# Decay attention and two expert layers: output products grouped by array tiling, a head pair's states stacked in 64 columns

## Chip, cores and metric

One core of one Trainium2 chip. The metric is device microseconds for one execution of the whole program. Before the change: median 974.29 us of 3 runs (974.17 to 976.9).

## The reference, cut to what matters

```python
# q, k, v, alpha: (batch 4, heads 8, seq 768, head_dim 48)
for t in range(S):
    state = alpha[:, :, t, :, None] * state + einsum('bhd,bhde', k[:, :, t], v[:, :, t])
    y[:, :, t] = einsum('bhd,bhde->bhe', q[:, :, t], state)
x = y.transpose(0, 2, 1, 3).reshape(3072, 384)
h = x @ w_in                                   # 384 -> 2048
x = (max(h, 0) + alpha_moe * min(h, 0)) @ w_out
h = x @ w_in2                                  # second layer, another activation g
out = g(h) @ w_out2
```

The weights arrive as float64. The expert layers multiply in two-part float32r words; the attention multiplies in float32.

## The kernel before, in words

**Attention.** The 768 tokens of a batch are cut into six chunks of 128 tokens (`CPB`), 24 chunks in all (`NCH`), numbered c = 0 to 23. A chunk holds all 8 heads, as 4 pairs (`NP`): the first head of a pair stands on partitions 0 to 47, the second on 64 to 111 (`HALVES`), and 48 to 63 and 112 to 127 are padding. Per chunk there are these parts:

- `fetch(c)`: q, k and the decays, transposed so that features stand on partitions, into `T`. Chunks 0 to 9 are transposed on TensorE (L195). Later ones are transposed on VectorE in blocks of 32 (`X`, L205), and sixteen DMAs put the blocks in place (`T<-X`, L211); then `load_chunk` loads the next chunk's inputs (L157).
- `at_alpha`: two scans over the decays, one backward (`R`, L221) and one forward (`F`, L226). `at_qk`: `K2` and `Q2`.
- `at_scores`: `sc`, one product a head with 48 rows (L247), masked into `A` by VectorE (L252), and `kt`, the transposed keys (L258), copied to `KT` by ScalarE (L260).
- `at_out`: the output `y` of the chunk, `[128, 4 pairs, 128 tokens]` in one PSUM tile. For each pair it is the product of the state `bd` with `Q2` (L271, left out in the first chunk of a batch) and for each head of the pair the product of `v` with `A` (L274). `bd` is block diagonal, 128 rows by 128 columns a pair, so that one product serves both heads. `ds` is the chunk's addition to the state (L288, left out in a batch's last chunk). ScalarE and VectorE then split `y` into the two float32r parts of `xs` (L300 to L307), and VectorE adds `ds` to `bd` (`state()`, L313 or L315), one instruction for each half. Six DMAs put the last pair's rows into the padding of the other three pairs (`xs<-x`, L323).
- `at_decay`: GpSimd multiplies `bd` by the next chunk's decays (L332), one instruction for each half.

**Startup.** Chunks 0 to 3, whose outputs are the first block of 512 tokens, run before any expert product. There `at_out` makes pair 3 first, ScalarE copies it (`y3`, L280), and three products with `sel` (L295) put its rows into the other pairs' padding, each behind its own pair. `mid()` stands between: ScalarE's copy of a weight (`split_hi`, L407).

**Expert layers.** Six blocks of 512 tokens for each layer, 16 steps (fc) a block: step s emits `hp` (L429, 9 products), the activation on VectorE and ScalarE (L444 to L452), the low part `gl` on GpSimd (L453), and then step s-1's output products (`o`, L462, 9 products in layer 0; `y`, L473 in layer 1). In the first block each step also loads, converts and splits a weight (VectorE `wf`, L366 and L368; ScalarE `wst`, L360 and L361).

**Order.** Every engine runs its instructions in the order in which the program emits them (`tc.manual_schedule`). After each step `run_slots` emits the next group of attention work: at_out(c-1); at_qk, at_decay and fetch; at_alpha; at_scores. Four steps make a chunk, so the attention of block j+1 is spread over block j, and the first `hp` of a block needs the last `xs` of its four chunks. All DMAs are issued by SyncE, one queue in program order.

The lines of `at_out` and `at_decay` that the change touches:

```python
        def emit_y(p, done=True):
            if not first:
                nc.tensor.matmul(out=y[:, p, :], lhsT=bd[:, p, :], rhs=s["Q2"][:, p, :],
                                 start=True, stop=False)
            for a in range(2):
                nc.tensor.matmul(out=y[64 * a:64 * a + 64, p, :], lhsT=vc[:, 2 * p + a, :],
                                 rhs=s["A"][a][:, p, :], start=first, stop=done)
```

Of the kernel before, what the change touches and what calls it, by code (L numbers as in the profile page):

```python
# [7 lines left out]
F32 = mybir.dt.float32  # L8
# [14 lines left out]
def kernel(  # L23
# [13 lines left out]
    nc = tc.nc  # L37
    B, H, S, D = q.shape
    NT, DM = out.shape
    DFF = w_in1.shape[1]  # L40
    P = 128
    C = 128
    NP = H // 2
# [40 lines left out]
    bd = const.tile([P, NP, P], F32, name="bd")  # L84
# [10 lines left out]
    def spare_tile(key, shape, name):  # L95
        """A tile of the startup in the place of a weight tile that comes later."""
        if key not in own:
            own[key] = wpool.tile(shape, F32, tag=next(spare), name=name)
        return own[key]

    def shared_row(g):
        """Where the last two heads' sixteen features g stand in their own tile."""
        return 16 * g if g < 3 else 64 + 16 * (g - 3)
# [60 lines left out]
    def flag(src, i, col):  # L164
        """Sums, into a column, how far the decays lie outside one end of the chunked form's range."""
        junk = p1.tile([P, 768], mybir.dt.uint8, tag="junk", name="junk")
        nc.scalar.activation(junk[:, 0:src.shape[1]], src, AF.Relu, scale=(-1.0, 1.0)[i],
                             bias=bias2[:, i:i + 1], accum_out=acc[:, col:col + 1])
# [8 lines left out]
    def load_flags(i):  # L177
        """The decays of the first batches, whose chunks pass without their flags."""
        t = p3.tile([P, 768], F32, tag="wst", name="al", padded_shape=[P, 4 * DM])
        nc.sync.dma_start(out=t, in_=alpha[i // NFL].rearrange("h t d -> (h t d)")  # L180
                          .rearrange("(p n) -> p n", p=P)[:, i % NFL * 768:(i % NFL + 1) * 768])
        own["al", i] = t
# [79 lines left out]
    def at_out(c, xdst, startup=False, mid=None):  # L262
# [6 lines left out]
        def emit_y(p, done=True):  # L269
            if not first:  # L270
                nc.tensor.matmul(out=y[:, p, :], lhsT=bd[:, p, :], rhs=s["Q2"][:, p, :],  # L271
                                 start=True, stop=False)
            for a in range(2):
                nc.tensor.matmul(out=y[64 * a:64 * a + 64, p, :], lhsT=vc[:, 2 * p + a, :],  # L274
                                 rhs=s["A"][a][:, p, :], start=first, stop=done)

        if startup:
            emit_y(ND)
            y3 = spare_tile(("y3", c % 2), [P, C], "y3")
            nc.scalar.copy(out=y3, in_=y[:, ND])  # L280
        else:
            for p in range(NP):
                emit_y(p)
        if not last:
            ds = pool.tile([P, NP, D], F32, tag=tag, name="ds", padded_shape=[P, NP, P])
            for h in range(H):
                lo = HALVES[h % 2][0]
                nc.tensor.matmul(out=ds[lo:lo + D, h // 2, :], lhsT=s["KT"][:, h // 2, lo:lo + D],  # L288
                                 rhs=vc[:, h, 0:D], start=True, stop=True)
        if mid:  # L290
            mid()
        if startup:
            for p in range(ND):
                emit_y(p, False)
                nc.tensor.matmul(out=y[:, p, :], lhsT=sel[:, p, :], rhs=y3, start=False, stop=True)  # L295
# [13 lines left out]
        def state():  # L309
            for l, r in HALVES:  # L310
                nv = bd[l:r, :, l:r]
                if first:
                    nc.vector.tensor_copy(out=nv, in_=ds[l:r])  # L313
                elif not last:
                    nc.vector.tensor_add(out=nv, in0=ds[l:r], in1=nv)  # L315
# [10 lines left out]
    def at_decay(c):  # L326
        """The state before chunk c, divided by the chunk's decays: block diagonal, by pairs."""
        if c % CPB:
            R = st[c]["R"]
            for lo, hi in HALVES:  # L330
                nv = bd[lo:hi, :, lo:hi]
                nc.gpsimd.tensor_mul(out=nv, in0=nv, in1=R[lo:hi, :, 0:1].to_broadcast([D, NP, D]))  # L332

# [24 lines left out]
    def words_f32(lo, hi, t, nbias):  # L358
        """lo, hi: the words of the float64 t, scaled so that the exponent is rebased."""
# [3 lines left out]
    def join_f32(f, lo, hi):  # L363
        """f: the float of the high word shifted by three, its sign, and the low word's top bits."""
# [175 lines left out]
    with tc.manual_schedule():  # L540
# [87 lines left out]
        # startup: the attention of the first block, chunks overlapped  # L628
# [91 lines left out]
def general_attention(tc, q, k, v, alpha, xT_d):  # L720
    """The recurrence itself, a scan over time for each column of the state: any decay."""
# [58 lines left out]
def general_layer(tc, layer, x_src, w_in, w_out, m_alpha, dst, B, to_f32):  # L780
    """One expert layer in float32 products, 128 tokens at a time."""
# [100 lines left out]
```

## Time and profile before

| what | value |
|---|---|
| timed runs | 974.29, 976.9, 974.17 us; median 974.29 |
| profiled execution, span from first to last instruction | 972.0 us |
| median of the runs less that span (launch and end, around the span) | 2.3 us |
| TensorE matmul busy | 941.8 us, 97% of the span |
| VectorE, ScalarE, GpSimd busy | 569.1 (59%), 350.6 (36%), 374.2 us (38%) |
| granted TensorE clock | full in nearly all of the 40 slices |

The profile of one execution gives its span; its own time is not listed apart from the three runs. Matmuls are pipelined, and their rows overlap: what a group of them costs is read from the start of one group to the start of the next, not from their durations. A float32 product is issued as two passes, so a row with "x4" holds two of the program's products. Busy shares are means over stages with different limits, so a stage's own table, its chain and its waits come first.

### The profile page before, as it was taken

The numbers are of one execution on the slowest core, as the hardware profiler recorded it, in microseconds if no ns is written. First come the engines' busy times: TensorE is split into PE (matmuls) and PEld (weight loads), VectorE is DVE, ScalarE is ACT, GpSimd is POOL, SyncE is SP. The second block draws the span as 40 slices with busy tenths as digits, with TensorE's granted clock in tenths as the row PEclk, the third lists the DMA queues.
The fourth block names the chain that finished last, engine by engine and source line by source line (L and its number), as shares of the span: only waits on it lengthen the run. The fifth ranks groups of instructions, "written<-read, shape, count | busy, mean of one in ns | idle before, by whom it ended". The sixth has DMA issues, their size and how long they took to land.

```text
span 972.0 us, 14041 instructions
## 1 busy us (share of the span) xinstructions
PE 941.8 (97%) x5219; PEld 788.0 (81%) x5219; DVE 569.1 (59%) x776; ACT 350.6 (36%) x590; POOL 374.2 (38%) x310
## 2 busy tenths in 40 slices
PE   7898889999999999999999999999999999999996
PEld 6676667777877778778778889999999999999995
DVE  8788887777867777776533433434434334344333
ACT  3544443232332323333223343345533333333332
POOL 3454454344333334433337853323333332233331
PEclk9999999999999999999999999999999999999999
DMA  9976637666766766674123320022000100100001
GB/s 180 189 160 134 137 70 153 144 132 126 154 130 128 151 152 162 133 155 116 39 92 122 107 71 11 1 92 71 24 32 11 55 0 11 55 12 1 33 1 37
DMA packets 227597, 87.15 MB, mean 90 GB/s; under 512 B 194736, under 2 KB 213952, under 8 KB 227520
## 3 DMA queue, kind: packets, MB, share of 16 engines
q1 hardware_dynamic: 227520, 86.16, 38.9%
q8 instruction: 43, 0.70, 0.3%
q14 instruction: 34, 0.28, 0.1%
HBM read 57.42 MB, written 15.73 MB: 75 GB/s over the span
## 4 chain that ended last, share of the span: by engine, by line
PE 82%; DVE 7%; SPq 4%; DMA 4%; issue 2%; ACT 2%; POOL 0%; DVEq 0%; ACTq 0%; POOLq 0%
PE hp L429 37%; PE y L473 20%; PE o L462 17%; PE y L274 2%; PE y L271 2%; PE sc L247 2%; DMA wst<-in_moe_w_in_dram 1%; SPq L157 1%; DVE wf L366 1%; DVE wf L368 1%; DMA wst<-in_moe_w_out_dram 1%; DVE g L444 1%; PE kt L258 1%; SPq L352 1%; DMA xs<-x 1%
## 5 line engine op out<-in xcount | busy, mean ns | idle before, releaser
L453 POOL TENSOR_TENSOR gl<-g,gh 128x512 fp32r<-128x512 f32 x191 | 263.8, 1381 | 505.2 <-ACT gh L452 450.7
L429 PE MATMUL hp<-xs,wh 128*128 128x512 f32 x1152 | 362.0, 396 | 1.3 <-DVE xs L305 0.8
L452 ACT CAST gh<-g 128x512 fp32r<-128x512 f32 (+1 forms) x193 | 119.3, 618 | 425.4 <-DVE g L446 273.7
L429 PEld LDWEIGHTS hp<-xs,wh 128*128 128x128 f32 x1152 | 211.6, 188 | 40.6 <-DVE T L185 0.9
L429 PE MATMUL hp<-xs,wl 128*128 128x512 f32 x576 | 226.7, 394 | 0.0
L449 DVE SCALAR_TENSOR_TENSOR g<-g 128x512 f32<-128x512 f32 (+1 forms) x97 | 68.3, 704 | 214.7 <-ACT g L441 213.2
L429 PEld LDWEIGHTS hp<-xs,wl 128*128 128x128 f32 x576 | 108.4, 188 | 23.1
L441 ACT ACTIVATE g<-hp,half 128x512 f32<-128x512 f32 (+1 forms) x97 | 66.1, 683 | 104.7 <-PE hp L429 101.4
L444 DVE TENSOR_SCALAR g<-hp,malpha 128x512 f32<-128x512 f32 x96 | 71.2, 742 | 55.5 <-PE hp L429 55.3
L462 PE MATMUL o<-gl,wh 128*128 128x512 f32 x288 | 83.5, 399 | 8.0 <-POOL gl L453 7.9
L462 PE MATMUL o<-gh,wh 128*128 128x512 f32 x288 | 83.1, 397 | 7.5 <-ACT gh L452 5.3
L473 PE MATMUL y<-wh,gh 128*128 128x384 f32 x384 | 83.4, 337 | 0.2
L473 PE MATMUL y<-wh,gl 128*128 128x384 f32 x384 | 83.0, 337 | 0.0
L473 PE MATMUL y<-wl,gh 128*128 128x384 f32 x384 | 82.6, 336 | 0.0
L462 PE MATMUL o<-gh,wl 128*128 128x512 f32 x288 | 82.3, 394 | 0.0
L473 PEld LDWEIGHTS y<-wh,gh 128*128 128x128 f32 x384 | 69.5, 188 | 9.1 <-ACT gh L452 1.0
L462 PEld LDWEIGHTS o<-gl,wh 128*128 128x128 f32 x288 | 53.6, 190 | 23.8 <-POOL gl L453 12.9
L462 PEld LDWEIGHTS o<-gh,wh 128*128 128x128 f32 x288 | 53.3, 188 | 23.1 <-ACT gh L452 9.8
L451 DVE TENSOR_TENSOR g<-hp,g 128x512 f32<-128x512 f32 (+1 forms) x97 | 66.5, 686 | 3.4
L446 DVE SCALAR_TENSOR_TENSOR g<-hp,g 128x512 f32<-128x512 f32 x96 | 66.4, 692 | 3.3
L473 PEld LDWEIGHTS y<-wh,gl 128*128 128x128 f32 x384 | 67.9, 188 | 0.4 <-DVE gl L453 0.3
L473 PEld LDWEIGHTS y<-wl,gh 128*128 128x128 f32 x384 | 68.0, 188 | 0.0
(97 smaller groups left out, 930.9 us busy)
## 6 DMA issues: line engine op xcount, KB each, us to landing
wst<-in_moe_w_out_dram SPq DMA_DIRECT2D x32, 384.0 KB, 4.8
T<-X SPq DMA_DIRECT2D x224, 48.0 KB, 2.1
wst<-in_moe_w_in_dram SPq DMA_DIRECT2D x16, 384.0 KB, 5.5
w_d<-wf SPq DMA_DIRECT2D x16, 384.0 KB, 5.6
w<-w_d SPq DMA_DIRECT2D x16, 384.0 KB, 3.0
wst<-in_moe_w_in_dram SPq DMA_DIRECT2D x32, 144.0 KB, 3.4
x_d<-ev SPq DMA_DIRECT2D x18, 256.0 KB, 4.5
x2s<-x_d SPq DMA_DIRECT2D x18, 256.0 KB, 3.0
```

Source lines behind the costliest of these rows:

```text
L247: nc.tensor.matmul(out=scs[h % 2][:, h // 2, :], lhsT=s["K2"][lo:lo + D, h // 2, :], rhs=s["Q2"][lo:lo + D, h // 2, :], start=True, stop=True)
L271: nc.tensor.matmul(out=y[:, p, :], lhsT=bd[:, p, :], rhs=s["Q2"][:, p, :], start=True, stop=False)
L429: nc.tensor.matmul(out=hp, lhsT=w[:, p, :], rhs=xs[:, x, p, :], start=(i == 0), stop=(i == 3 * ND - 1))
L441: nc.scalar.activation(y, x, AF.Relu, bias=half, scale=0.5)
L444: nc.vector.tensor_scalar(out=y, in0=x, scalar1=0.0, scalar2=malpha[:, fc:fc + 1], op0=ALU.min, op1=ALU.mult)
L446: nc.vector.scalar_tensor_tensor(out=y, in0=x, scalar=0.0, in1=y, op0=ALU.max, op1=ALU.add)
L449: nc.vector.scalar_tensor_tensor(out=y, in0=y, scalar=1.0, in1=y, op0=ALU.min, op1=ALU.mult)
L451: nc.vector.tensor_max(out=y, in0=x, in1=y)
L452: nc.scalar.copy(out=hi, in_=y)
L453: (nc.gpsimd if parts == 1 else nc.vector).tensor_sub(out=lo, in0=y, in1=hi.bitcast(F32))
L462: nc.tensor.matmul(out=ops[d], lhsT=w[:, d * P:(d + 1) * P], rhs=g, start=first, stop=last)
L473: nc.tensor.matmul(out=ops[t], lhsT=g[:, t * P:(t + 1) * P], rhs=w, start=first, stop=last)
```

## The change

It makes all state products of a chunk first and all products with `A` after them, in place of a state product and two products with `A` pair by pair. `bd` has 64 columns a pair instead of 128: the first head's state stands on rows 0 to 47, the second's on 64 to 111, both in columns 0 to 47. So a state product has 48 rows and 64 columns, and there are two a pair, one for each half, at opposite corners of the array. In the startup the copy `y3` and the products with `sel` follow all of them. `ds` is made with 64 columns of `KT` instead of 48, so that the padding rows are written (with zeros), and the state's addition and decay take all 128 partitions in one instruction instead of two of 48. The opening marks on PSUM (`start`) stand on the first products of a bank alone.

```diff
-    bd = const.tile([P, NP, P], F32, name="bd")
+    bd = const.tile([P, NP, 64], F32, name="bd")
@@ at_out
-        def emit_y(p, done=True):
+        def emit_ys(done):
             if not first:
-                nc.tensor.matmul(out=y[:, p, :], lhsT=bd[:, p, :], rhs=s["Q2"][:, p, :],
-                                 start=True, stop=False)
-            for a in range(2):
-                nc.tensor.matmul(out=y[64 * a:64 * a + 64, p, :], lhsT=vc[:, 2 * p + a, :],
-                                 rhs=s["A"][a][:, p, :], start=first, stop=done)
+                for p in range(NP):
+                    for lo, hi in HALVES:
+                        nc.tensor.matmul(out=y[lo:lo + 64, p, :], lhsT=bd[lo:hi, p, :],
+                                         rhs=s["Q2"][lo:hi, p, :], start=p == 0, stop=False,
+                                         skip_group_check=True)
+            for p in range(NP):
+                for a in range(2):
+                    nc.tensor.matmul(out=y[64 * a:64 * a + 64, p, :], lhsT=vc[:, 2 * p + a, :],
+                                     rhs=s["A"][a][:, p, :], start=first and p == 0, stop=done,
+                                     skip_group_check=True)
+        emit_ys(not startup)
         if startup:
-            emit_y(ND)
             y3 = spare_tile(("y3", c % 2), [P, C], "y3")
             nc.scalar.copy(out=y3, in_=y[:, ND])
-        else:
-            for p in range(NP):
-                emit_y(p)
         if not last:
...
-                nc.tensor.matmul(out=ds[lo:lo + D, h // 2, :], lhsT=s["KT"][:, h // 2, lo:lo + D],
+                nc.tensor.matmul(out=ds[lo:lo + 64, h // 2, :], lhsT=s["KT"][:, h // 2, lo:lo + 64],
                                  rhs=vc[:, h, 0:D], start=True, stop=True)
         if mid:
             mid()
         if startup:
             for p in range(ND):
-                emit_y(p, False)
                 nc.tensor.matmul(out=y[:, p, :], lhsT=sel[:, p, :], rhs=y3, start=False, stop=True)
@@ state
-            for l, r in HALVES:
-                nv = bd[l:r, :, l:r]
+            nv = bd[:, :, 0:D]
@@ at_decay
-            for lo, hi in HALVES:
-                nv = bd[lo:hi, :, lo:hi]
-                nc.gpsimd.tensor_mul(out=nv, in0=nv, in1=R[lo:hi, :, 0:1].to_broadcast([D, NP, D]))
+            nv = bd[:, :, 0:D]
+            nc.gpsimd.tensor_mul(out=nv, in0=nv, in1=st[c]["R"][:, :, 0:1].to_broadcast([P, NP, D]))
```

TensorE at `at_out` of a chunk inside the expert steps (chunk 7, the same in every later chunk with a state and an addition to it): `o` are the previous step's output products, `hp` the next step's. Before:

```order
L462 MATMUL o_637<-gl,wh_1149 128x512
L271 MATMUL y<-Q_1261,bd 128x128
L274 MATMUL y<-A,vt 64x128 x2
L271 MATMUL y<-Q_1261,bd 128x128
L274 MATMUL y<-A,vt 64x128 x2
L271 MATMUL y<-Q_1261,bd 128x128
L274 MATMUL y<-A,vt 64x128 x2
L271 MATMUL y<-Q_1261,bd 128x128
L274 MATMUL y<-A,vt 64x128 x2
L288 MATMUL ds<-vt,KT 48x48 x8
L429 MATMUL hp<-xs,wh_1290 128x512 x2
```

And of the change:

```order
L463 MATMUL o_642<-gl,wh_1159 128x512
L275 MATMUL y<-Q_1270,bd 64x128 x8
L280 MATMUL y<-A,vt 64x128 x8
L292 MATMUL ds<-vt,KT 64x48 x8
L430 MATMUL hp<-xs,wh_1298 128x512 x2
```

The four state products became eight of half the columns and stand in one row; the eight with `A` follow in one row; nothing else moved.

TensorE at `at_out` of chunk 2 in the startup (`sc` and `kt` are the scores and keys of this chunk ahead of it, of chunk 3 behind it). Before:

```order
L258 MATMUL kt<-ident,K_346 128x128 x4
L271 MATMUL y<-Q_347,bd 128x128
L274 MATMUL y<-A,v_147 64x128 x2
L288 MATMUL ds<-v_147,KT 48x48 x8
L271 MATMUL y<-Q_347,bd 128x128
L274 MATMUL y<-A,v_147 64x128 x2
L295 MATMUL y<-y_298,sel 128x128
...
L247 MATMUL sc<-Q_268,K_267 128x128 x8
```

And of the change:

```order
L258 MATMUL kt<-ident,K_344 128x128 x4
L275 MATMUL y<-Q_345,bd 64x128 x8
L280 MATMUL y<-A,v_147 64x128 x8
L292 MATMUL ds<-v_147,KT 64x48 x8
L298 MATMUL y<-y_304,sel 128x128 x3
L247 MATMUL sc<-Q_268,K_267 128x128 x8
```

Three rounds of state, `A` and `sel` stood behind `ds`; now only the three products with `sel` do, and pair 3, from which they are fed, ends last.

VectorE at the same `at_out` of chunk 2, before:

```order
L366 SCALAR_TENSOR_TENSOR wf<-wst 128x768
L368 SCALAR_TENSOR_TENSOR wf<-wst,wf 128x768
L315 TENSOR_TENSOR bd<-ds,bd 48x4x48 x2
L305 TENSOR_TENSOR xs<-y,xs 128x3x128
L252 TENSOR_TENSOR A<-sc,mask 128x512 x2
```

And of the change:

```order
L367 SCALAR_TENSOR_TENSOR wf<-wst 128x768
L369 SCALAR_TENSOR_TENSOR wf<-wst,wf 128x768
L318 TENSOR_TENSOR bd<-ds,bd 128x4x48
L309 TENSOR_TENSOR xs<-y,xs 128x3x128
L252 TENSOR_TENSOR A<-sc,mask 128x512 x2
```

One addition is gone there, and in every chunk but a batch's last; GpSimd loses one decay in every chunk but a batch's first.

## Rows read from the trace of the kernel before

**Rows 1.** By stage: bounds, us; busy PE, PEld, DVE, ACT, POOL; clock; DMA share; GB/s.
```profile
0.00:41.00 41.00, 34.82 (x306) 26.37 (x306) 31.95 (x60) 16.53 (x28) 16.20 (x39) 1.00 1.07 190
41.00:155.00 114.00, 98.13 (x565) 72.91 (x566) 98.76 (x115) 53.79 (x82) 58.48 (x39) 0.99 0.61 128
155.00:283.00 128.00, 128.00 (x767) 101.94 (x767) 96.89 (x131) 40.53 (x77) 46.49 (x40) 1.00 0.69 144
283.00:432.00 149.00, 148.34 (x891) 117.44 (x890) 113.08 (x154) 49.12 (x94) 54.96 (x46) 1.00 0.69 145
```

**Rows 2.** Timeline, TensorE, at_out of chunk 8: start, length (us), operation.
```profile
163.84 0.85 PE L462 MATMUL o<-gl,wh 128*128 128x512 f32 x3
164.53 0.38 PE L271 MATMUL y<-Q,bd 128*128 128x128 f32 x2
164.84 0.44 PE L274 MATMUL y<-A,vt 128*64 128x128 f32 x4
...
167.47 0.53 PE L288 MATMUL ds<-vt,KT 128*48 128x48 f32 x16
167.93 0.72 PE L429 MATMUL hp<-xs,wh 128*128 128x512 f32 x2
```

**Rows 3.** Timeline, TensorE, at_out of chunk 12, first of its batch, without state products.
```profile
249.88 0.85 PE L462 MATMUL o<-gl,wh 128*128 128x512 f32 x3
250.66 1.09 PE L274 MATMUL y<-A,vt 128*64 128x128 f32 x16
251.58 0.53 PE L288 MATMUL ds<-vt,KT 128*48 128x48 f32 x16
```

**Rows 4.** Timeline, TensorE, at_scores of chunk 9: the products with 48 rows.
```profile
180.50 1.16 PE L247 MATMUL sc<-Q,K 48*128 48x128 f32 x16
181.59 0.66 PE L258 MATMUL kt<-ident,K 128*128 128x128 f32 x4
```

**Rows 5.** Groups by line and form: weight loads of 64 and of 48 columns.
```profile
L274 PEld LDWEIGHTS y<-A,vt 128*64 128x64 f32 x336 | 16.8, 135 | 10.0 <-issue 0.7 <-DVE wf L366 0.4 <-ACT y L280 0.3
L288 PEld LDWEIGHTS ds<-vt,KT 128*48 128x48 f32 x272 | 8.7, 125 | 0.0
```

**Rows 6.** Timeline, VectorE, startup, from chunk 2's masks to chunk 3's.
```profile
27.83 1.29 DVE L252 TENSOR_TENSOR A<-sc,mask 128x512 f32<-128x512 f32 x2
...
30.62 0.96 DVE L368 SCALAR_TENSOR_TENSOR wf<-wst,wf 128x768 uint32<-128x768 uint32 x1
32.58 0.74 DVE L315 TENSOR_TENSOR bd<-ds,bd 48x192 f32<-48x192 f32 x2 [1.00 <-PE y L271]
33.81 0.56 DVE L305 TENSOR_TENSOR xs<-y,xs 128x384 fp32r<-128x384 f32 x1 [0.49 <-ACT xs L300]
34.38 1.29 DVE L252 TENSOR_TENSOR A<-sc,mask 128x512 f32<-128x512 f32 x2
```

**Rows 7.** Timeline, ScalarE, the same stretch: the weight's copy and the output's.
```profile
31.61 0.83 ACT L407 CAST wh<-wf 128x768 fp32r<-128x768 f32 x1 [1.70 <-DVE wf L368]
33.30 0.48 ACT L300 CAST xs<-y 128x384 fp32r<-128x384 f32 x1 [0.85 <-PE y L295]
```

**Rows 8.** The chain from 50 to 150 us: the state's additions on it.
```profile
73.03 0.36 DVE bd L315
...
142.28 0.36 DVE bd L315
```

**Rows 9.** Timeline, SyncE: from the issue of one chunk's T<-X to the next one's.
```profile
389.14 10.53 SPq L211 DMA_DIRECT2D T<-X  x16
...
405.01 3.82 SPq L323 DMA_DIRECT2D xs<-x  x6
...
410.01 1.25 SPq L211 DMA_DIRECT2D T<-X  x2
```

**Rows 10.** Timeline, VectorE: the wait for chunk loads ahead of their transposition.
```profile
279.54 1.78 DVE L205 STREAM_TRANSPOSE X<-nat 128x1536 f32<-128x1536 f32 x1 [1.26 <-DMA nat<-in_q_dram]
```

**Rows 11.** Timeline, TensorE: the first product of the fifth block.
```profile
410.80 0.70 PE L429 MATMUL hp<-xs,wh 128*128 128x512 f32 x2 [0.55 <-DMA xs<-x]
```

More of the change, by code (lines that the diff above doesn't have):

```diff
@@ L293, in at_out @@
             for p in range(ND):
-                emit_y(p, False)
-                nc.tensor.matmul(out=y[:, p, :], lhsT=sel[:, p, :], rhs=y3, start=False, stop=True)
+                nc.tensor.matmul(out=y[:, p, :], lhsT=sel[:, p, :], rhs=y3, start=False, stop=True,
+                                 skip_group_check=True)
         xs, o = xdst
@@ L309, in state @@
         def state():
-            for l, r in HALVES:
-                nv = bd[l:r, :, l:r]
[L312 to L315, printed above, removed]
+            nv = bd[:, :, 0:D]
+            if first:
+                nc.vector.tensor_copy(out=nv, in_=ds)
+            elif not last:
+                nc.vector.tensor_add(out=nv, in0=ds, in1=nv)
         for f in (state, low) if startup else (low, state):
@@ L328, in at_decay @@
         if c % CPB:
-            R = st[c]["R"]
-            for lo, hi in HALVES:
-                nv = bd[lo:hi, :, lo:hi]
-                nc.gpsimd.tensor_mul(out=nv, in0=nv, in1=R[lo:hi, :, 0:1].to_broadcast([D, NP, D]))
+            nv = bd[:, :, 0:D]
+            nc.gpsimd.tensor_mul(out=nv, in0=nv, in1=st[c]["R"][:, :, 0:1].to_broadcast([P, NP, D]))
     wt = {}
```

## Prediction

> **What bounds the kernel.** I read the stage table first, since busy shares of the whole span hide where TensorE waits. Until 41 us the DMA engines are full (share 1.07) and TensorE works 34.8 of 41 us; from 41 to 155 us TensorE works 98.1 of 114 us and VectorE is as busy (98.8); from 155 to 432 us TensorE never stops, 128.0 of 128 and 148.3 of 149 us [rows 1]. So a product saved in the third and fourth stage shortens the run unless something else is then late, while one saved in the second is covered by VectorE and the weights' conversion. The timeline of TensorE in one chunk of the third stage comes next: from the start of the last `o` group to `ds` it is 167.47 - 163.84 = 3.63 us [rows 2]. There each change between the full array (`bd`) and half the columns (`A`) is a break, and there are seven. A batch's first chunk makes no products with `bd` and shows what `A` costs in one piece: 0.78 us from the start of the `o` group to its first product, 0.92 us from there to `ds` [rows 3]. Last I read VectorE and ScalarE in the startup [rows 6, 7], the chain in the second stage [rows 8] and SyncE's queue [rows 9].
>
> **State products, third and later stages.** They turn from four of 128 rows and 128 columns into eight of 48 rows and 64 columns at opposite corners. The trace has no product of this form. The two nearest are `A`, half the columns, 16 passes in 0.92 us up to `ds` [rows 3], and `sc`, half the rows, 16 passes in 1.09 us up to the next arrangement [rows 4]. In both, 16 passes take the time of 8, so the two halves of a pair run side by side. I take 1.02 us for the state block: the `A` block, which it is nearest to in columns, and a change of arrangement behind it, which the 1.09 us contain and the 0.92 do not. The bounds are 0.92 and 1.09. The new sum is 0.78 + 1.02 + 0.92 = 2.72 us against 3.63: 0.91 us less a chunk. Chunks 8 to 23 are in these stages, less the first chunks 12 and 18: 14 chunks, 12.7 us.
>
> **A rule against it.** The kernel before keeps the two halves of `sc` in two PSUM tiles; the change lets both row halves of the state write one tile, in different partitions, and no run here shows that. The Trainium skill, TensorEngine Tiling (Array Packing), section Restrictions and Gotchas, says that different row tiles cannot access the same PSUM bank at once. By that rule the pairs would go one after the other, and the time would be the first rival's. What hangs on it: I give it little, because the halves write different partitions, as the two halves of `A` and of `ds` do, and those share a tile and run side by side [rows 2, 3].
>
> **ds.** Its weights grow from 48 to 64 columns; the moving side stays. The loads of 64 columns take 135 ns, those of 48 take 125 [rows 5]. If a load sets the pace of each of the 8 pairs, that is 8 x 10 = 80 ns a chunk; if the products hide it, nothing; if the pace goes with the columns, a third of the present 167.93 - 167.47 = 0.46 us [rows 2], 0.15. I take 0.08 for 13 chunks (8 to 22 without 11 and 17, which have no `ds`): 1.0 us lost.
>
> **What is late next.** With 0.83 us less in a chunk, SyncE's queue comes close. From one chunk's `T<-X` to the next it takes 410.01 - 389.14 = 20.87 us; 22 issues (16 + 6) take 10.53 + 3.82 = 14.35 us [rows 9], 0.65 each, so the 29 of a chunk (16 `T<-X`, 3 loads, 3 for weights, 6 `xs`, 1 for `v`) take 18.9, and every fourth chunk has three more for an evicted block. TensorE would need 20.0. Two places already wait for this queue: VectorE's transposition 1.26 us for its loads [rows 10], with the activations of the next step queued behind it, and the fifth block's first product 0.55 us for `xs` [rows 11]. In the stage from 283 to 432 us six shortened chunks (14 to 17, 19, 20) should gain 5.0 us. Nothing is lost if the slack takes it, all 5.0 if SyncE keeps its pace. No row says where between; I take half, 2.5 us. Before 283 us I take nothing off, since TensorE had no such wait there [rows 1], and after chunk 20 no more `T<-X` are issued.
>
> **Startup.** Chunk 2 takes 34.38 - 27.83 = 6.55 us on VectorE, of which it waits 1.00 us for `y` and 0.49 us for ScalarE's copy [rows 6]. With the state, `A` and `sel` products in three blocks TensorE is done earlier, and another chain is left: masks, keys and weight to 30.62 + 0.96 = 31.58 [rows 6], 3.75 us; then the weight's copy 0.83 and the output's 0.48 on ScalarE [rows 7], which stand in that order; then `xs` 0.56 [rows 6]. With some 0.1 us between them that is 5.7 us, 0.8 less. One addition (0.36) falls away inside. The new wait is for `y3`, behind the last product with `A`; `ds` (0.46 us) covers most of it. The bounds are 0, if the full DMA engines [rows 1] set the pace, and 1.85 us (both waits and one addition). I take 0.8 for each of four chunks: 3.2 us.
>
> **Second stage.** The shorter `y` of chunks 4, 5 and 7 is covered by VectorE: nothing. But one addition of 0.36 us falls away in chunks 4, 6 and 7 and stands on the chain each time, of which the first and the last are shown [rows 8]: 1.0 us. An instruction over 128 partitions with the same 192 elements in each costs as much as one over 48, I assume; if it cost two, this term is nothing. GpSimd's second decay is worth nothing: GpSimd is busy 46.5 of 128 us [rows 1]. If that cover failed it would matter ahead of `gl`, as half a microsecond in a few steps.
>
> **The sum.** 12.7 - 1.0 - 2.5 + 3.2 + 1.0 = 13.4 us less. The profiled span of 972.0 us becomes 958.6; the median of the runs is 2.3 us above that span, so 974.3 becomes **960.9 us**.
>
> **Rivals.**
> - *The halves do not run side by side.* 16 passes then take twice 0.92, 1.84 us, and a chunk 3.54 against 3.63: 0.09 x 14 = 1.3 us, less 1.0 for `ds`, with 1 us of the startup (chunk 0 makes no products with `bd`) and 1.0 of the second stage: 972 us. For it: no row has two row halves in one tile. Against: `sc` and `A` each run in pairs [rows 3, 4]. The rule of the Trainium skill named above would give this. Chance 0.09.
> - *SyncE's queue takes the stage from 283 to 432 us.* The whole 5.0 us go: 963.4 us. For it: the two waits [rows 10, 11]. Against: the estimate of 18.9 us. Chance 0.22.
> - *The startup is paced by its loads.* Its 3.2 us go: 964.1 us. For it: the share of 1.07. Against: VectorE's waits name `y` and its copy, not a load [rows 6]. Chance 0.15.
> - *Slower: every change of corner drains the array.* A pair of passes lasts 0.38 us with a pitch near 0.11 [rows 2], so one alone lasts 0.27. Sixteen without overlap are 4.3 us; a chunk takes 0.78 + 4.3 + 0.92 = 6.0 against 3.63. 14 x 2.4 = 33 us and some 7 in the startup: 1014 us. It decides from 3.63 - 0.78 - 0.92 = 1.93 us for the block, 0.12 us a pass. For it: every change of arrangement in chunk 8 is a break [rows 2]. Against: `A` and `sc` change halves at each product without one [rows 3, 4]. Chance 0.04.
>
> **How the numbers follow.** The forecast as summed has 0.47, and 0.03 lies below it. The range takes in the second and third rival. Downwards: no loss at SyncE 2.5, the state block at 0.92 another 1.4, `ds` free 1.0, and 1 us more of the startup: 955. Upwards: all of SyncE's loss 2.5, the block at 1.09 another 1.0, `ds` at 0.15 another 0.9 and half the startup, 1.6: 967. About 0.82 lie inside: 0.22 + 0.15 and nearly all of the forecast's 0.47. A measurement of this kernel tells about 0.3%, 2.9 us, from no change. Faster by more than that: 0.88. Within it: the first rival, mostly, 0.08. Slower: 0.04.
>
> **What would show it.** From the `o` group to `ds` in chunk 8: 2.7 us if right, 3.5 or 6.0 if a rival is. `ds` to the next `hp`: 0.46 to 0.6 us. The first `hp` of the first block near 37.8 us, where now the startup's stage ends at 41 [rows 1]; TensorE's idle time from 283 to 432 us, now 0.7 us, near 3; SyncE's next `T<-X` without a gap ahead of it. The forecast is wrong if the state block is over 1.2 us, if the startup ends past 40, or if TensorE idles more than 6 us in the fourth stage.

## The result and the profile after

| | before | after |
|---|---|---|
| timed runs | 974.29, 976.9, 974.17, 978.37 us | 964.38, 965.63, 963.51, 966.87 us |
| median | 975.6 us | 965.0 us |
| ratio of after to before | | 0.9893, 95% interval 0.987 to 0.9917 |
| profiled execution, span | 972.0 us | 962.7 us (its own time 964.38) |
| TensorE matmul busy | 941.8 us | 925.7 us |
| VectorE, GpSimd busy | 569.1, 374.2 us | 558.6, 363.4 us |

The forecast was 960.9 us, 955 to 967. The time lies inside the range and 4.1 us above the forecast. TensorE's busy time fell by 16.1 us and the span by only 9.3. Where the first `hp` of each block of 16 steps starts, in both traces, shows where the rest went (times in us; the third row of numbers is the difference):

| | step 1 | 17 | 33 | 49 | 65 | 81 | end |
|---|---|---|---|---|---|---|---|
| before | 40.97 | 154.59 | 240.63 | 325.57 | 410.80 | 496.93 | 972.0 |
| after | 37.05 | 148.07 | 232.03 | 319.27 | 404.43 | 487.20 | 962.7 |
| after less before | -3.92 | -6.52 | -8.60 | -6.30 | -6.37 | -9.73 | -9.3 |

The gain grows up to step 33, falls by 2.3 us in the next block, stands still in the one after, and grows again from step 65 to step 81. The third and the fourth stage of the changed kernel (columns as in [rows 1]; the bounds follow the work, so they lie some microseconds earlier):

```profile
148.00:275.00 127.00, 125.88 (x815) 101.63 (x813) 94.11 (x126) 40.30 (x77) 44.27 (x35) 1.00 0.70 145
275.00:425.00 150.00, 144.51 (x935) 116.14 (x935) 111.10 (x149) 48.78 (x94) 52.37 (x41) 0.99 0.71 143
```

TensorE, which was never idle in the third stage and 0.7 us in the fourth [rows 1], now idles 1.1 and 5.5 us there. So the work was saved, and waits took part of its place.

The timeline of TensorE at `at_out` of chunk 8, which answers to [rows 2]:

```profile
157.32 0.85 PE L463 MATMUL o<-gl,wh 128*128 128x512 f32 x3
158.10 1.09 PE L275 MATMUL y<-Q,bd 48*64 48x128 f32 x16
159.12 1.09 PE L280 MATMUL y<-A,vt 128*64 128x128 f32 x16
160.04 0.62 PE L292 MATMUL ds<-vt,KT 128*64 128x48 f32 x16
160.60 0.72 PE L430 MATMUL hp<-xs,wh 128*128 128x512 f32 x2
```

From `o` to `ds` it is 160.04 - 157.32 = 2.72 us, where it was 3.63. The state block takes 159.12 - 158.10 = 1.02 us for 16 passes. `ds` to `hp` grew from 0.46 to 0.56 us. Every later chunk with a state and an addition repeats this to within 0.01 us.

The waits of the first `hp` at three block starts, TensorE's timeline (the wait and its releaser stand in brackets):

```profile
232.03 0.71 PE L430 MATMUL hp<-xs,wh 128*128 128x512 f32 x2 [1.12 <-DMA xs<-x]
...
319.27 0.71 PE L430 MATMUL hp<-xs,wh 128*128 128x512 f32 x2 [2.25 <-DMA xs<-x]
...
404.43 0.70 PE L430 MATMUL hp<-xs,wh 128*128 128x512 f32 x2 [1.63 <-DMA xs<-x]
```

Before there was one such wait, of 0.55 us [rows 11]. SyncE's queue ahead of the longest of them, from one chunk's `T<-X` to the next's:

```profile
296.99 11.33 SPq L211 DMA_DIRECT2D T<-X  x16
308.42 0.55 SPq L157 DMA_DIRECT2D nat<-in_alpha_dram  x1
309.01 0.60 SPq L157 DMA_DIRECT2D nat<-in_k_dram  x1
309.66 0.86 SPq L157 DMA_DIRECT2D nat<-in_q_dram  x1
310.56 1.29 SPq L355 DMA_DIRECT2D wst<-in_moe_w_in_dram  x1
311.90 1.53 SPq L356 DMA_DIRECT2D wst<-in_moe_w_out_dram  x1
313.53 0.38 SPq L399 DMA_DIRECT2D w_d<-wf  x1
314.02 3.96 SPq L326 DMA_DIRECT2D xs<-x  x6
318.08 0.53 SPq L162 DMA_DIRECT2D vt<-in_v_dram  x1
...
318.71 3.90 SPq L211 DMA_DIRECT2D T<-X  x6
```

And VectorE, in the same stretch and one chunk earlier:

```profile
272.46 1.78 DVE L205 STREAM_TRANSPOSE X<-nat 128x1536 f32<-128x1536 f32 x1 [3.41 <-DMA nat<-in_q_dram]
...
309.71 0.28 DVE L311 TENSOR_TENSOR x<-y,x 128x128 fp32r<-128x128 f32 x1
```

The 29 issues take 21.03 us with 0.69 us of gaps between them: 318.71 - 296.99 = 21.72 us. TensorE needs 20.6 us a chunk where nothing holds it up (82.1 to 82.7 us for four, in the first experiment below). VectorE had the rows of `xs` ready at 309.99, and their DMAs were issued from 314.02 on, 4.03 us later, behind three loads of inputs and three weight transfers. The inputs come late as well: the load of q for the transposition at 272.46 was issued behind sixteen `T<-X`, and VectorE waited 3.41 us for it, with the activations of the step behind it.

### The profile page after: what moved, and what is told of

Same layout as the page of the kernel before. It is cut to its first block, busy times and chain, and to the rows that moved or that the text cites. A ratio compares the mean times of both kernels' runs of the same rounds, so it can differ in the third digit from the quotient of the medians.

```text
span 962.7 us, 14310 instructions
## 1 busy us (share of the span) xinstructions
PE 925.7 (96%) x5379; PEld 781.9 (81%) x5379; DVE 558.6 (58%) x756; ACT 349.8 (36%) x590; POOL 363.4 (38%) x290
## 4 chain that ended last, share of the span: by engine, by line
PE 76%; DVE 9%; DMA 5%; SPq 4%; issue 3%; ACT 2%; POOL 0%; DVEq 0%; ACTq 0%; POOLq 0%
PE hp L430 34%; PE y L474 20%; PE o L463 14%; PE sc L247 2%; PE y L280 2%; PE y L275 1%; DVE wf L367 1%; DVE g L445 1%; DMA xs<-x 1%; DVE wf L369 1%; DVE g L447 1%; SPq L211 1%; DMA nat<-in_k_dram 1%; PE kt L258 1%; DMA wst<-in_moe_w_out_dram 1%
```

## The experiments

Theory: SyncE's one queue became the bound between 150 and 430 us; what stands in it and in what order is what the lost time comes from. Main rival: the transfers themselves, on shared DMA engines. Side questions: is it the grouping or the stacked state that saves the time, and what are the startup and the single addition worth.

### Five issues a chunk to another queue

```diff
-                load_chunk(n, nc.sync)
+                load_chunk(n, nc.scalar if c >= NPE else nc.sync)
...
-            if 0 <= i + 1 < NFC:
-                load_w(1, i + 1, nc.sync)
             if 0 <= i < NFC:
                 conv_w(1, i)
                 store_w(i)
+            if 0 <= i + 1 < NFC:
+                load_w(1, i + 1, nc.scalar)
```

> The changed kernel, with five of SyncE's 29 issues of a chunk given to ScalarE's queue: the three loads of the next chunk's inputs and the two loads of a second-layer weight. The same transfers, the same products. Theory (SyncE's queue of issues is the bound from about 150 to 430 us): the issues of a chunk fall from some 21 us to about 17, under TensorE's 20; the waits of the first `hp` of a block for `xs<-x` (1.12, 2.25, 1.63 us in the changed kernel) fall under 0.3 us each, VectorE's wait of 3.4 us ahead of a transposition goes, the half-speed stretch behind the 2.25 us wait goes too, and the time is 957 to 960 us, some 6 us under the changed kernel's 965.0. Rival 1 (the transfers themselves are late, because the DMA engines are shared by inputs, weights and blocks): the waits stay within 1 us of 5.0 in sum and the time within 1.5 us of 965. Rival 2 (ScalarE has no room for issues): `xs` waits go, but TensorE waits for `gh` instead, over 3 us between 150 and 430 us, and the time is 963 or more.

Measured: 956.35 us (956.26 to 958.73), ratio to before 0.98, interval 0.9785 to 0.9816; the span is 954.4 us. The block starts, TensorE's timeline:

```profile
316.42 0.71 PE L430 MATMUL hp<-xs,wh 128*128 128x512 f32 x2 [0.20 <-issue]
...
396.82 0.62 PE L430 MATMUL hp<-xs,wh 128*128 128x512 f32 x2
```

SyncE's queue in the same stretch:

```profile
294.39 13.75 SPq L211 DMA_DIRECT2D T<-X  x16
308.24 0.55 SPq L399 DMA_DIRECT2D w_d<-wf  x1
308.90 4.76 SPq L326 DMA_DIRECT2D xs<-x  x6
```

The first row lies inside the first step of the fourth block, which started at 314.69; the second is the start of the fifth, without a wait. From step 17 to step 81 it is 479.51 - 149.46 = 330.05 us; the changed kernel took 487.20 - 148.07 = 339.13. The products are the same and so are the bytes. So the first rival falls, and ScalarE had the room: TensorE waited for `gh` nowhere between 150 and 430 us. The row of `T<-X` holds waits now (13.75 us for what took 11.33), so SyncE has room, and one issue stands between it and `xs` where six did. The Trainium skill, Perfetto Trace Analysis, section DMA Optimizations, says that where an issuing engine's own track is the bottleneck, balancing the transfers over several issuing engines may help; this run agrees, by the 9 us between the ratios 0.9893 and 0.98.

The same edit on the kernel before:

> The kernel before with the same five issues a chunk moved from SyncE to ScalarE. Theory: the kernel before was bound by TensorE there and had one wait of 0.55 us for `xs`, so nothing over 1 us is to be had: 974 to 976 us beside 975.6. Rival (SyncE's queue already set its pace, or the move helps by itself, by earlier loads): it gains as the changed kernel does, 3 us or more.

Measured: 973.99 us (973.04 to 974.99), ratio 0.9972, interval 0.9963 to 0.9982: 2.7 us gained by the ratio, more than the 1 us expected; the interval is 1.8 to 3.6 us and takes in the rival's 3. The profiled execution of before shows one wait of 0.55 us for this queue [rows 11]; the timed runs on that chip lie between 974.6 and 980.7 us, those with the edit within 2 us of each other. That fits a kernel that was already at the edge of this queue and fell behind it in some executions, but no profile of such an execution was taken. The second layer's time differs by as much among the kernels profiled here (last section), so the cause of the 2.7 us stays open.

### The inputs first, all on SyncE

```diff
-    def at_in(c):
+    def at_in(c, nxt):
         nc.vector.transpose(out=X, in_=nat.rearrange("t x h d -> t (x h d)"))
+        nxt()
         X5 = X.rearrange("t (n a r i) -> t n a r i", n=NS, a=2, r=2)
```

`nxt` issues the next chunk's three loads, which stood behind `at_in`.

> The changed kernel, all issues still on SyncE, but from chunk 10 on the three loads of the next chunk's inputs stand ahead of the sixteen `T<-X` and not behind them; ScalarE's range flags of a chunk stand ahead of both. Same number of issues. Theory (the sum of the issues is the bound, some 21 us a chunk): VectorE's wait of 3.4 us for inputs goes, as they are asked for 11 us sooner, but the waits for `xs<-x` at the block starts stay, 3 to 6 us in sum, and the time is 961 to 965. Rival (late inputs hold up VectorE and with it the queue, so their place is what matters): the `xs` waits fall under 1 us in sum and the time comes to 957 to 960, as with five issues moved to ScalarE.

Measured: 961.92 us, ratio 0.985, interval 0.981 to 0.989, which still overlaps that of the change (0.987 to 0.9917). TensorE waits at two block starts, 3.13 and 0.95 us; the longer one:

```profile
317.78 1.19 PE L431 MATMUL hp<-xs,wh 128*128 128x512 f32 x2 [3.13 <-DMA xs<-x]
```

As the theory had it: the order seems to give back part (from 150 to 430 us VectorE's transposition waits for no input, though 4.8 us for the `T<-X` before it, which read the same buffer), the waits for `xs` stay at 4.1 us, and the rest of the loss needs fewer issues.

### Four issues more

```diff
+        for i in range(4):
+            nc.sync.dma_start(out=scrap[:, i:i + 1], in_=w0[0:P, i:i + 1])
```

> The changed kernel with four more issues on SyncE behind each chunk's `T<-X`, from chunk 10 to 23: loads of 4 bytes to each of 128 partitions, 2 KB together in a chunk, into a tile that nothing reads. Theory (the number of SyncE's issues sets the pace): each takes 0.4 to 0.65 us, so 1.6 to 2.6 us a chunk; with nothing to spare in the queue, 12 chunks up to 430 us cost 17 to 30 us: 982 to 995. Rival 1 (the bytes on the DMA engines set it): 2 KB are nothing, 965 within 2 us. Rival 2 (the queue has slack between its issues): 965 to 972.

Measured: 990.23 us, ratio 1.0133, interval 1.0089 to 1.0177. TensorE at one of three block starts with such a wait:

```profile
240.86 1.19 PE L434 MATMUL hp<-xs,wh 128*128 128x512 f32 x2 [5.75 <-DMA xs<-x]
```

And the added issues of one chunk on SyncE:

```profile
299.86 2.03 SPq L215 DMA_DIRECT2D scrap<-in_v_dram  x4
```

Twelve chunks by 2.03 us are 24 us; by the ratios (1.0133 and 0.9893) 23 us were lost, for transfers of 2 KB a chunk. Issues are the price, not bytes; whether the price of one goes with its pieces (128 of 4 bytes here) no run separates. The same issues with the five others moved:

> The same four extra issues a chunk on SyncE, with the five others on ScalarE: 28 issues of some 19 us for TensorE's 20.6. Theory: they find room, 956 to 959 us. Rival (any issue costs its time): 17 us or more above 956.

Measured: 978.05 us, ratio 0.9998, interval 0.9974 to 1.0021. The expectation fell: the span is 976.5 us, 22.1 longer than with the five issues moved alone, although the queue has room in the sum. SyncE ahead of one block start:

```profile
303.69 11.71 SPq L212 DMA_DIRECT2D T<-X  x16
315.44 3.19 SPq L215 DMA_DIRECT2D scrap<-in_v_dram  x4
318.74 0.38 SPq L403 DMA_DIRECT2D w_d<-wf  x1
319.22 4.05 SPq L329 DMA_DIRECT2D xs<-x  x6
```

VectorE's last part of `xs`, and TensorE's wait inside that block's first step:

```profile
314.62 0.28 DVE L314 TENSOR_TENSOR x<-y,x 128x128 fp32r<-128x128 f32 x1
```

```profile
325.13 0.70 PE L434 MATMUL hp<-xs,wh 128*128 128x512 f32 x2 [2.14 <-DMA xs<-x]
```

The rows were ready at 314.90 and were issued at 319.22, behind the sixteen `T<-X` of a later chunk and whatever stands after those. So the sum is only half of the theory: the place of `xs` in the queue, behind `T<-X`, leaves it little slack, and an issue put between them delays the block's start even when the queue is idle elsewhere in the chunk. TensorE's waits in the first steps of three blocks come to 8.6 us of the 22 (2.26 and 0.58, 2.14 and 0.87, 1.28, 1.24 and 0.26), and two stretches at half clock follow them. Step by step beside the run with five issues moved alone, the steps at these block starts, half clock included, lose 4.8, 5.7 and 3.6 us; four steps in which TensorE waits for late activations lose 4.2; and 3.3 come behind step 81, where a block of the second layer takes 66.67 us in place of 66.35 (last section). That is 21.6 of the 22.1 us.

### Grouping or stacking

The grouping alone, with the block diagonal of before:

```diff
-                    for lo, hi in HALVES:
-                        nc.tensor.matmul(out=y[lo:lo + 64, p, :], lhsT=bd[lo:hi, p, :],
-                                         rhs=s["Q2"][lo:hi, p, :], start=p == 0, stop=False,
-                                         skip_group_check=True)
+                    nc.tensor.matmul(out=y[:, p, :], lhsT=bd[:, p, :], rhs=s["Q2"][:, p, :],
+                                     start=p == 0, stop=False, skip_group_check=True)
```

> The changed kernel's grouping alone: all state products first, then all with `A`, but the state block diagonal as before, 128 rows by 128 columns a pair, four products of two passes, with two additions, two decays and `ds` of 48 columns. Theory (the breaks between arrangements cost, not the width): the block before had 1.93 us for 4 state products and 7 breaks; 8 passes at a pitch of 0.11 are 0.85 us, with one break about 1.0, so from the `o` group to `ds` 2.6 to 2.8 us, as in the changed kernel (2.73), `ds` to `hp` back to 0.46 us, and the time within 2 us of 965, the second additions (0.36 us in some chunks of the second stage) against the cheaper `ds`. Rival (the half-width products side by side bring the gain): 3.2 us or more from `o` to `ds`, and a time of 968 to 971 us.

Measured: 966.71 us, ratio 0.9895, interval 0.9875 to 0.9914. TensorE in chunk 8:

```profile
161.09 0.85 PE L463 MATMUL o<-gl,wh 128*128 128x512 f32 x3
161.78 1.05 PE L274 MATMUL y<-Q,bd 128*128 128x128 f32 x8
162.76 1.09 PE L278 MATMUL y<-A,vt 128*64 128x128 f32 x16
163.69 0.53 PE L290 MATMUL ds<-vt,KT 128*48 128x48 f32 x16
164.14 0.73 PE L430 MATMUL hp<-xs,wh 128*128 128x512 f32 x2
```

2.60 us from `o` to `ds` and 0.45 on to `hp`: 3.05, where the change has 3.28. Eight full passes take 0.98 us with the break behind them, sixteen half ones 1.02; and between `o` and a full-width block there is no break (0.69 us, against 0.78). TensorE's gain is the grouping's. The time is no better than the change's, although a chunk takes 0.23 us less: the second additions and decays are back, which cost VectorE (below), and in this profiled execution, the slowest of four, the second layer took 478.95 us against the changed kernel's 475.50 (last section). Stacking, the other way round:

```diff
-            if not first:
-                for p in range(NP):
+            for p in range(NP):
+                if not first:
                     for lo, hi in HALVES:
...
-            for p in range(NP):
                 for a in range(2):
```

> The changed kernel with the stacked state in 64 columns, but the products pair by pair again: two state products, then two with `A`, four times. Theory (a change between 128 and 64 rows breaks the stream as one between 128 and 64 columns does, 0.15 us each, seven of them): from the `o` group to `ds` 0.78 + 1.02 + 0.92 + 7 x 0.15 less the one change already counted, 3.5 to 3.8 us, no better than before (3.63); the time within 3 us of 972, its startup still better by the `y3` order. Rival (only leaving the full array costs, since both forms have 64 columns): 2.7 to 2.9 us, and a time within 1.5 us of 965.

Measured: 977.51 us (974.03 to 978.84), ratio 0.9999, interval 0.9984 to 1.0015. TensorE in chunk 8:

```profile
160.17 0.85 PE L462 MATMUL o<-gl,wh 128*128 128x512 f32 x3
160.95 0.44 PE L275 MATMUL y<-Q,bd 48*64 48x128 f32 x4
161.32 0.44 PE L279 MATMUL y<-A,vt 128*64 128x128 f32 x4
161.69 0.44 PE L275 MATMUL y<-Q,bd 48*64 48x128 f32 x4
...
163.79 0.62 PE L291 MATMUL ds<-vt,KT 128*64 128x48 f32 x16
```

3.62 us, as before the change. Each four passes take 0.37 us where four grouped ones take 0.23 (`A`) or 0.26 (state), so a change between 48 and 128 rows breaks the stream as the one between 64 and 128 columns did. TensorE's gain in these chunks was gone. The time lies above the 969 to 975 us expected. In the profiled execution, the slowest of ten, step 17 starts at 150.92 us, 3.67 ahead of the kernel before; then steps 17 to 81 take 347.11 us against 342.34, with waits of 0.60 and 1.17 us for `xs` and 1.62 for `gh`; and the second layer, which the edit does not touch, takes 4.0 us longer (last section). So the ratio of 1 is not the price of the lost grouping alone.

### The startup and the single addition

The startup's products in the order of before, with the stacked state (`emit_y` makes one pair):

```diff
-        emit_ys(not startup)
+        if startup:
+            emit_y(ND, True)
+        else:
+            emit_ys(True)
...
             for p in range(ND):
+                emit_y(p, False)
```

> The changed kernel, but in the startup the products stand in the order of before: pair 3 first, its copy, `ds`, then each pair's state and `A` products followed by its product with `sel`. The stacked state and all later chunks are as in the changed kernel. Theory (the startup's gain of some 3.9 us, first `hp` at 37.05 in place of 40.97 us, counts in full, because all queues start later with it): first `hp` of the first block at 40.5 to 41.5 us and a time of 968 to 970 us, 3 to 5 above the changed kernel's 965.0. Rival (SyncE's queue sets the pace later anyway, and its loads do not start earlier with the startup): the time is within 1.5 us of 965.0.

Measured: 970.95 us (967.43 to 973.94), ratio 0.9936, interval 0.9912 to 0.996; the time is just above the 970 us expected. The first `hp` starts at 42.80 us, later than expected and 1.8 us later than before the change. The 5.75 us lost against the changed kernel's 37.05 are still there at step 17 (153.82 against 148.07) and in the span (969.2 against 962.7). The startup counts in full, and the rival falls.

Two additions and two decays:

```diff
-            nv = bd[:, :, 0:D]
+            for l, r in HALVES:
+                nv = bd[l:r, :, 0:D]
...
```

> The changed kernel with the state's addition and its decay each in two instructions of 48 partitions, as before; the products are the changed ones. Theory (three additions of 0.36 us stood on the chain of the second stage, and an instruction over 128 partitions costs what one over 48 does): the 17th step's first `hp`, at 148.07 us in the changed kernel, comes 0.7 to 1.5 us later, and the time is 965.5 to 967. Rival (VectorE has room for them): 148.1 within 0.3 us and a time within 0.5 us of 965.0.

Measured: 967.59 us, ratio 0.9899, interval 0.9861 to 0.9937, by time not to be told from the change. The trace tells more, TensorE's first `hp` of the first and of the 17th step:

```profile
37.95 0.74 PE L432 MATMUL hp<-xs,wh 128*128 128x512 f32 x2 [0.94 <-DVE xs L309]
...
151.64 0.62 PE L432 MATMUL hp<-xs,wh 128*128 128x512 f32 x2
```

The startup is 0.90 us longer than in the changed kernel's execution (37.05); but with the changed startup the first `hp` comes at 37.05 to 37.75 us in different executions, so how much of it the three additions cost there stays open. Between the two rows it is 113.69 us against the changed kernel's 111.02, 2.67 more, and the 17th step starts 3.57 us later, where 0.7 to 1.5 was expected. The kernel before took 113.62. This execution had a stretch at half clock near 48 us and the changed kernel's had none, but that is not the reason: the run with the old startup and the run with the inputs first, which are the changed kernel in these steps, had such a stretch too and took 111.03 and 111.08 us.

Beside the run with the old startup, instruction by instruction, VectorE falls back in two places, three times each: by 0.52 to 0.56 us at a second addition (0.36, and what it delays), and by 0.31 at a second decay. GpSimd and VectorE in this run, then in the changed kernel:

```profile
53.37 1.54 POOL L335 TENSOR_TENSOR bd<-bd,R 48x192 f32<-48x192 f32 x2
54.48 1.25 DVE L369 SCALAR_TENSOR_TENSOR wf<-wst 128x768 uint32<-128x768 uint32 x1
...
52.44 0.96 POOL L333 TENSOR_TENSOR bd<-bd,R 128x192 f32<-128x192 f32 x1
53.55 0.94 DVE L367 SCALAR_TENSOR_TENSOR wf<-wst 128x768 uint32<-128x768 uint32 x1
```

While GpSimd works on the second decay, VectorE's `wf` takes 1.25 us in place of 0.94, here and at the next two decays. So the stacked state's single addition and single decay are worth 2.6 us in the second stage, 1.6 by VectorE's additions and 0.9 by GpSimd's decays. One addition over 128 partitions takes 0.35 us, one over 48 takes 0.35.

### Versions that beat both

The five issues on ScalarE's queue and the full-width grouping together, the two edits above:

> Both that proved good alone: the five issues a chunk on ScalarE's queue, and the products grouped with the state block diagonal and full width as before (two additions, two decays, `ds` of 48 columns). From the `o` group to `hp` it takes 2.594 us in place of 2.822 in a chunk with state and addition, 0.13 less in a batch's last and 0.09 less in its first: over chunks 8 to 23 that is 11 x 0.228 + 3 x 0.13 + 2 x 0.09 = 3.1 us less than 956.35. The second additions cost 1.0 us in the second stage, the startup's chunk 3 up to 0.9. Theory: 953.5 to 956 us. Rival (the additions and the startup cost as much as the products give): 956.4 or more.

Measured: 956.48 us (956.07 to 958.17), ratio 0.9791, interval 0.9762 to 0.9819; by the intervals not to be told from the moved issues alone (0.98), and where the rival had it. It gains 1.9 us from step 17 to 81 (328.15 against 330.05), less than the 3.1 expected, and loses 2.8 ahead of step 17 (152.25 against 149.46), where the second additions and decays cost.

So each form where it is cheaper, with the five issues on ScalarE, and beside it the first experiment once more:

```diff
+    WIDE = 2 * CPB
...
+            if not first and c >= WIDE:
+                for p in range(NP):
+                    nc.tensor.matmul(out=y[:, p, :], lhsT=bd[:, p, :], rhs=s["Q2"][:, p, :],
+                                     start=p == 0, stop=False, skip_group_check=True)
+            elif not first:
...
```

> Five issues a chunk on ScalarE's queue; the stacked 64-column state for chunks 0 to 11, where its single addition shortens VectorE's chain, and the grouped full-width block diagonal from chunk 12 on, where TensorE is the bound. Theory: chunks 12 to 23 take 8 x 0.228 + 2 x 0.13 + 2 x 0.09 = 2.3 us less than with the stacked state, and the startup and the second stage keep their gain: 954 us where the stacked state with the same relief is 956.35. Rival (the second additions on VectorE or the decays on GpSimd delay the transposition and `gl` there as well): within 0.7 us of the stacked state with relief in the same comparison.

> The changed kernel with five issues a chunk on ScalarE's queue, a second time, so that the mixed form is compared with it on one chip: 956 to 957 us.

Measured on one chip: 953.88 us (952.67 to 956.11), ratio 0.9762, interval 0.9733 to 0.979, beside 957.21 us (955.51 to 960.44), 0.9803, 0.9775 to 0.9831. The mixed form has the lower median by 3.3 us, but the intervals overlap: its lead over the moved issues alone is likely, not shown. Both are well below the change.

## Why the prediction was right, and where not

| term | forecast | measured |
|---|---|---|
| startup | 3.2 | 3.9 |
| second stage, additions | 1.0 | 2.6: additions 1.6, decays 0.9 (by the run with two of each) |
| state products, chunks 8 to 23 | 12.7 | 14 x 0.90 = 12.6 |
| `ds` | -1.0 | 13 x 0.09 = -1.2 |
| what is late next | -2.5 | -8.5 |
| second layer | 0 | -0.4 |
| sum | 13.4 | 9.0 (the spans differ by 9.3) |

**State products and `ds`: right, to a tenth.** The block between `A` and `sc` was the right guess (1.02 us taken, 1.02 measured), and the weights' columns did set part of `ds`. The forecast's reason, that breaks and not width cost, held in both single edits. Two rivals fall with the 1.02 us: the halves run side by side, and no change of corner drains the array. By the rule of the Trainium skill, TensorEngine Tiling (Array Packing), section Restrictions and Gotchas, that different row tiles cannot access one PSUM bank at once, the block should have taken 1.84 us; the trace does not agree, with two row halves writing one tile in 1.02 us.

**Startup: right in kind.** The first `hp` came at 37.05, not 37.8; loads did not pace it, since the order of products alone moves it by 5.75 us.

**Second stage: mis-sized, with one term wrongly at nothing.** The additions did stand on VectorE's chain, but the stage gained 2.6 us and not 1.0: each of the three cost over 0.5 us, not 0.36, and the second decay, which the text put at nothing because GpSimd is idle enough, lengthened VectorE's `wf` by 0.31 us three times. The share given for it (46.5 of 128 us) is the third stage's; in the second it is 58.48 of 114 [rows 1]. Idle time on GpSimd was the wrong question: what counted was VectorE's instruction beside it. The stretch at half clock near 50 us, which only the execution before had, takes no part: by the eighth step the changed kernel, without one, and the run with the old startup, with one, lie 49.00 and 49.02 us behind their first `hp`.

**What is late next: the step that failed**, by size and by stage. It put all of the 29 issues at 0.65 us, 18.9 us a chunk, from the `T<-X` and `xs` rows. Loads and weight transfers take 0.4 to 1.5 us, `T<-X` took 0.71, and gaps stand between: 21.7 us in the chunk shown. From one `T<-X` to the fourth after it, a block's eviction included, SyncE took 84.9 and 85.5 us before (239.57, 324.51, 410.01) and 87.3 and 85.0 us after (231.46, 318.71, 403.68), with hardly a wait for another engine's data left; TensorE, for which the step took 20.0 us a chunk, came to need 82.1 to 82.7 for four. The sentence "before 283 us I take nothing off, since TensorE had no such wait there" failed too. The likely reason is that SyncE was just in time there, and such a queue is late by what is saved elsewhere. From the starts of the `o` and `hp` rows the loss divides into 4.8 us of waits for `xs` (1.27, 2.41 and 1.80, less 0.71 of the wait before), 2.2 us behind the late inputs near 276 us, and 1.6 us of half clock behind the 2.25 us wait. The rival that gave 5.0 us to the queue was the nearer one and stopped at the fourth stage. TensorE idles 5.5 us in that stage, nearer to the 6 that the text gave as its sign of being wrong than to the 3 it expected.

**Where it was right by luck.** The startup's 0.7 and the second stage's 1.6 us hid part of the 6.0 us that the queue's term was short. The 0.7 is no more than what executions with this startup differ by.

## What to carry to other kernels

Group products by their arrangement before making them smaller: here the grouping alone gave TensorE's gain, and smaller tiles in turn with others gave it none. Before an instruction on an idle engine is put at nothing, look whether those beside it on the bound engine get longer. When a bound engine is shortened, sum every issue of the in-order queue that feeds it from its own rows, gaps included, and compare it with the bound engine over a whole cycle; if they are level, the queue eats what is saved, and moving a few issues to an idle engine's queue gives it back (here some 9 us by the ratios, 0.9893 to 0.98, on top of the change's own 1.1%). In such a queue look at what stands between a transfer's data being ready and its issue, since that delays it even when the queue has room in the sum.

## What the runs showed of the hardware

**A wait can cost twice, through the clock.** TensorE's granted clock after the 2.25 us wait, in windows of 2 us (bounds; busy PE, PEld, DVE, ACT, POOL; clock; DMA share; GB/s), changed kernel:

```profile
318.00:320.00 2.00, 0.73 (x3) 0.67 (x4) 1.84 (x4) 0.62 (x1) 1.10 (x1) 0.96 0.41 85
320.00:322.00 2.00, 2.00 (x6) 1.54 (x6) 1.91 (x1) 0.00 (x0) 0.83 (x1) 0.50 0.70 113
```

0.50 is the lower level, 1.2 GHz. The kernel before had the same after a wait of 1.99 us at its second step, TensorE's timeline:

```profile
48.69 1.16 PE L462 MATMUL o<-gh,wh 128*128 128x512 f32 x3 [1.99 <-ACT T L202]
...
53.69 0.48 PE L429 MATMUL hp<-xs,wh 128*128 128x512 f32 x1
```

The changed kernel at the same place, after a wait of 2.18 us:

```profile
44.97 0.96 PE L463 MATMUL o<-gh,wh 128*128 128x512 f32 x3 [2.18 <-ACT T L202]
...
48.38 0.48 PE L430 MATMUL hp<-xs,wh 128*128 128x512 f32 x1
```

The same nine products of `o` and twelve passes of transpositions take 5.00 us and 3.41 us: 1.59 us of TensorE's time for one such stretch. What the run loses depends on what bounds it: in this stage, with VectorE the bound, nothing was left of it by the eighth step, while behind the 2.25 us wait, with TensorE the bound, the 1.6 us stayed lost. Nor is it certain to come: the changed kernel with five issues moved had it after a wait of 3.79 us in one execution, and in another, after 2.75 us, the clock stayed full. So a difference of up to 1.6 us between two executions here need not come from the edit.

**Halves of a pair side by side gain nothing over a full product.** Sixteen passes of 48 rows by 64 columns in 1.02 us, eight of 128 by 128 in 0.98: the pairs do run together, but a full product already does both at once.

**GpSimd's work can lengthen VectorE's.** One `wf` takes 0.94 us alone and 1.25 while a 0.51 us decay runs on GpSimd, at three decays of the second stage (the run with two of each).

**The second layer's time differs at full clock.** From start to start, a block of 16 steps takes 66.35 us in most of the profiled executions, 66.67 in both runs with four extra issues, and 66.99 in the grouped full-width and the ungrouped run, all at a granted clock of 1.00; over the whole layer that is 2 to 4 us. None of these edits touches the layer, and the cause is open. Whoever compares two kernels here should compare this stretch first.
